# HGRN2 recurrence and SwiGLU block in fp32: the state of two heads kept as diagonal blocks over 128 rows

## The chip, the cores and the metric

The kernel runs on one core of a Trainium2 chip. The metric is the device time of one execution in microseconds (us); the figure of a kernel is the median of its runs.

## What is computed

Four sequences (batch) of 768 tokens, eight heads of 48 dimensions. Each head keeps a 48x48 state that is decayed by a gate f row by row and takes in the outer product of k and v; the output of a token is q times the state. The result, with the heads of a token side by side (384 columns, 3072 tokens), goes through a SwiGLU block with three weight matrices, which arrive in float64.

```python
q, k, v, f_logit: (4, 8, 768, 48)
f = 1.0 / (1.0 + np.exp(-f_logit))
for t in range(S):
    state = f[:, :, t, :, None] * state + np.einsum('bhd,bhe->bhde', k[:, :, t], v[:, :, t])
    y[:, :, t] = np.einsum('bhd,bhde->bhe', q[:, :, t], state)
x = y.transpose(0, 2, 1, 3).reshape(B * S, H * D)          # (3072, 384)
g = x @ w_gate                                             # (384, 1536)
out = (g * sigmoid(g) * (x @ w_val)) @ w_out               # (1536, 384)
```

## The kernel before

**Tiling.** The recurrence runs in chunks of 128 tokens, six per sequence, 24 in all (chunk u is sequence b = u // 6 and position c = u % 6). The main loop (L276 to L285) goes over the 24 chunks; `attention(u)` is a generator that yields twelve times. Three chunks make a block of 384 tokens for the SwiGLU part; `mlp(g)` returns fifteen pieces of work for block g (twelve `hidden`, three `down`), and the main loop runs one piece behind every second yield of the next block's chunks. The last chunk of a block gets only the three `down` pieces, in its first half. In chunks 0 to 2 the pieces are the eighteen conversions of float64 weights to fp32, which are work for DVE and one product on POOL. The order on each engine is set by the tile scheduler; TensorE fills what it can with the SwiGLU matmuls.

**One chunk.** Raw f, q and k stand as tokens x (8 heads x 64), the upper 16 of each 64 columns zero. Twelve transposes (L143) turn them so that two heads share the 128 partitions, rows 0 to 47 and 64 to 111, with zeros between; four such pairs (index a) lie side by side. POOL forms the products of neighbouring gates e (L193) and q times f (L168). L165 and, in seven levels, L185 form the weights A of token s in token t: 48-row matmuls, the two heads of a pair in rows 0 and 64. After a level's matmuls DVE multiplies half of qT (L188), POOL half of kT (L190) by gates, and DVE copies the level's part of the scores into A under a mask (L194). After the last level qT is q times all gates of the chunk up to the token.

**The y stage.** For each of the eight heads y is A times v (L205, a contraction over the chunk's 128 tokens) and, where c > 0, qT times the state before the chunk (L208, a contraction over the head's 48 rows). Both add up in the same PSUM columns. A head's two matmuls follow one another, so in these chunks TensorE changes between 128 rows and 48 rows at every matmul. The two heads of a pair write different PSUM banks. L210 (ACT) copies y to x.

**The state.** It is a tile of 128 x (4 pairs x 48). For chunks c < 5 kT is transposed back (L217), copied (L219) and multiplied by v into PSUM, dS (L221); DVE decays the old state (L226) and adds dS (L227), or only copies it for c = 0 (L229). Then x is transposed for the SwiGLU part (L240, L242). `hidden` is L253 to L258, `down` L263 to L268. Loads are issued by SyncE two chunks ahead.

Of the kernel before, what the change touches and what calls it, by code (L numbers as in the profile page):

```python
# [8 lines left out]
FP32 = mybir.dt.float32  # L9
# [3 lines left out]
ALU = mybir.AluOpType  # L13
# [3 lines left out]
def kernel(  # L17
# [10 lines left out]
):  # L28
    """Gated linear recurrence over chunks of 128 tokens, then a SwiGLU block, all in fp32.

    Within a chunk the weight of token s in token t is the product of the gates of s+1..t. It is
    formed level by level: at level m the chunk splits into blocks of 2m tokens, and pairs with s
    in a block's left half and t in its right half take (product from s to the middle) times
    (product from the middle to t). Both are products of gates, so nothing exceeds 1 whatever the
    gates are, and nothing is divided. From a level to the next, q's right halves and k's left
    halves take the product of the neighbour half's gates.

    Two heads share the partitions, 64 apart; the two parities of head use different PSUM banks.
    """
    nc = tc.nc  # L40
# [3 lines left out]
    HP = H // 2  # L44
# [19 lines left out]

# [1 line left out]
    ident = const.tile([128, 128], FP32, tag="ident", name="ident")  # L66
    make_identity(nc, ident)
    masks = {}
    for m in LEVELS:
        mk = const.tile([128, 64], I32, tag=f"mask{m}", name=f"mask{m}")  # L70
        # s - (first token of t's block of 2m): within [0, m) where s is in its left half
        nc.gpsimd.iota(mk, pattern=[[-2 * m, 64 // m], [0, m]], base=0, channel_multiplier=1)
        nc.vector.tensor_single_scalar(mk, mk, ~(m - 1), op=ALU.bitwise_and)
        nc.vector.tensor_single_scalar(mk, mk, 0, op=ALU.is_equal)
        masks[m] = mk
# [10 lines left out]

# [1 line left out]
    units = [(b, c) for b in range(B) for c in range(NCH)]  # L88
# [10 lines left out]
    def weight_pieces(dst, src):  # L99
        """Fills dst (fp32) from src in pieces. A float64 comes as two int32 words, low first, and  # L100
        is rounded to fp32 here: sign and exponent make a power of two (0 below fp32's normal
        range, inf above it), which takes 1 + the mantissa's two parts."""
        n0, n1 = dst.shape[1:]
# [24 lines left out]

# [1 line left out]
    state = {}  # L130
    xT = {}

    def rows_of(par):
        return slice(W * par, W * par + D)

    def attention(u):
# [21 lines left out]

        # s = t
        A = att.tile([128, H, C], FP32, tag="A", name="A")  # L160
# [11 lines left out]

        # s < t, level by level
        E = fT
# [24 lines left out]

        # y: within the chunk, and from the state before it  # L200
        y = aps.tile([128, 2, 512], FP32, tag="a", name="y")
        for a in range(HP):
            for par in range(2):
                o = y[:, par, a * D:(a + 1) * D]
                nc.tensor.matmul(o, lhsT=A[:, par * HP + a, :], rhs=vt[u][:, 2 * a + par, :], start=True, stop=(c == 0))  # L205
                if c:
                    r = rows_of(par)
                    nc.tensor.matmul(o, lhsT=qT[r, a, :], rhs=state[b, c - 1][r, a, :], start=False, stop=True)  # L208
        x = att.tile([128, HP, 2, D], FP32, tag="x", name="x")
        nc.scalar.copy(x.rearrange("t a r d -> t r a d"),  # L210
                       y[:, :, 0:HP * D].rearrange("t r (a d) -> t r a d", d=D))
        yield

        if c < NCH - 1:
            p = aps.tile([128, 2, 512], FP32, tag="a", name="dS")
            for a in range(HP):
                nc.tensor.transpose(p[:, 0, a * C:(a + 1) * C], kT[:, a, :], ident)  # L217
            kt = att.tile([128, H, W], FP32, tag="kt", name="kt")
            nc.scalar.copy(kt, p[:, 0].rearrange("t (h d) -> t h d", d=W))  # L219
            for h in range(H):  # L220
                nc.tensor.matmul(p[W * (h % 2):W * (h % 2) + W, 1, (h // 2) * D:(h // 2 + 1) * D],  # L221
                                 lhsT=kt[:, h, :], rhs=vt[u][:, h, :], start=True, stop=True)
            s = att.tile([128, HP, D], FP32, tag="state", name="state", bufs=3)
            dS = p[:, 1, 0:HP * D].rearrange("p (a d) -> p a d", d=D)
            if c:
                nc.vector.tensor_tensor(s, state[b, c - 1], E.broadcast_to((128, HP, D)), ALU.mult)  # L226
                nc.vector.tensor_tensor(s, s, dS, ALU.add)  # L227
            else:
                nc.vector.tensor_copy(s, dS)  # L229
            state[b, c] = s  # L230
        yield

        # x.T for the block of tokens
        g = u // GROUP
# [9 lines left out]

# [1 line left out]
    def mlp(g):  # L246
# [24 lines left out]

# [1 line left out]
    for u in range(AHEAD):  # L273
# [46 lines left out]
```

## Time and profile before

| | |
|---|---|
| median of 3 runs | 1224.22 us (1221.59 to 1225.0) |
| span of the profiled execution | 1223.5 us (the page gives no other time of it) |
| TensorE busy | 1104.9 us, 90% |
| VectorE (DVE), GpSimd (POOL), ScalarE (ACT) busy | 34%, 22%, 14% |

The span is from the first to the last instruction of one execution. PE is TensorE's matmuls and PEld its weight loads. An fp32 matmul stands as two records, so `x2` in the timeline is one matmul and `x16` eight; a transpose is one record. A duration in the timeline runs from the first start to the last end of a merged group; the pace is read from the starts, since the end of a matmul is modelled. PEclk is the clock that TensorE was granted, as a share of 2.4 GHz; it has two levels, 1.00 and 0.50, and a mean over a stretch can lie between.

### The profile page before, as it was taken

The page shows a single profiled execution, that of the slowest core. Times are in us where ns is not written, and L with a number is a line of the kernel's source. Part 1 is how long each engine was busy: PE and PEld are TensorE (multiplying, and loading weights), DVE is VectorE, ACT ScalarE, POOL GpSimd, SP SyncE. Part 2 cuts the span into 40 slices and gives each one's busy share as a digit, 9 for nine tenths or more (in the row PEclk, how much of TensorE's full clock was granted, in tenths as well). Part 3 has the DMA queues.
Part 4 walks back from the last instruction along what each step waited for, and adds up shares of the span by engine and source line. Part 5 has one row for each costly group of instructions (what it writes and reads, how often), then busy time and mean ns, then how long its engine had stood idle before and what let it go on. Part 6 is the DMA issues. An engine that isn't in the chain of part 4 may idle for free.

```text
span 1223.5 us, 14949 instructions
## 1 busy us (share of the span) xinstructions
PE 1104.9 (90%) x6264; PEld 761.0 (62%) x6264; DVE 421.3 (34%) x656; ACT 166.7 (14%) x288; POOL 267.4 (22%) x400
## 2 busy tenths in 40 slices
PE   3546599998999999998999989998999989998998
PEld 3545566666666576666666666665666666665654
DVE  5997952321432222421332222412232213322110
ACT  1101022010121011210121110210121110110010
POOL 3454331111221121311221221211221211211000
PEclk9955588896998978988898968989798969989799
DMA  9534211010011010110110110110110100000000
GB/s 196 130 113 113 68 26 27 1 39 19 15 27 26 20 27 7 20 33 13 27 27 7 33 33 1 27 26 20 27 27 1 40 7 1 1 1 20 1 1 19
DMA packets 106721, 38.69 MB, mean 32 GB/s; under 512 B 100512, under 2 KB 103584, under 8 KB 106656
## 3 DMA queue, kind: packets, MB, share of 16 engines
q1 hardware_dynamic: 103200, 33.04, 12.4%
q10 hardware_dynamic: 3456, 4.72, 1.1%
q8 instruction: 49, 0.80, 0.3%
q14 instruction: 16, 0.13, 0.0%
HBM read 33.03 MB, written 4.72 MB: 31 GB/s over the span
## 4 chain that ended last, share of the span: by engine, by line
PE 84%; DVE 11%; issue 3%; POOL 1%; ACT 0%; DMA 0%; SPq 0%; DVEq 0%; POOLq 0%; ACTq 0%
PE gate L253 17%; PE val L253 16%; PE o L263 15%; PE sc L185 14%; PE y L205 7%; PE y L208 7%; DVE A L194 3%; DVE qT L188 2%; PE fkT L143 2%; PE sc L165 2%; PE dS L221 1%; PE dS L217 1%; DVE p L116 1%; PE xTp L240 1%; PE qTp L143 1%
## 5 line engine op out<-in xcount | busy, mean ns | idle before, releaser
L185 PEld LDWEIGHTS sc<-qT,kT 48*128 48x128 f32 x2688 | 188.2, 211 | 156.9 <-issue 79.8
L185 PE MATMUL sc<-qT,kT 48*128 48x64 f32 x2688 | 211.6, 302 | 78.2 <-DVE A L194 56.3
L253 PE MATMUL gate<-xT,w_gate 128*128 128x384 f32 x576 | 244.2, 538 | 0.6 <-ACT xT L242 0.6
L253 PE MATMUL val<-xT,w_val 128*128 128x384 f32 x576 | 216.1, 514 | 0.0
L190 POOL TENSOR_TENSOR kT<-kT,e 128x256 f32<-128x256 f32 x144 | 118.1, 820 | 393.4 <-PE sc L185 393.4
L263 PE MATMUL o<-w_out,h 128*128 128x384 f32 x576 | 197.0, 493 | 1.1 <-ACT ob L266 1.1
L253 PEld LDWEIGHTS val<-xT,w_val 128*128 128x128 f32 x576 | 117.6, 204 | 86.1 <-issue 14.6
L258 DVE TENSOR_TENSOR h<-silu,val 128x384 f32<-128x384 f32 x96 | 53.2, 554 | 317.5 <-PE val L253 317.5
L263 PEld LDWEIGHTS o<-w_out,h 128*128 128x128 f32 x576 | 105.8, 190 | 69.8 <-ACT ob L266 2.4
L194 DVE COPY_PREDICATED A<-mask,sc 128x512 f32<-128x512 int32 x168 | 147.0, 875 | 0.0
L188 DVE TENSOR_TENSOR qT<-qT,e 128x256 f32<-128x256 f32 x144 | 63.3, 440 | 213.4 <-PE sc L185 213.1
L253 PEld LDWEIGHTS gate<-xT,w_gate 128*128 128x128 f32 x576 | 101.4, 200 | 45.2 <-issue 4.4
L205 PE MATMUL y<-v,A 128*128 128x48 f32 x384 | 99.5, 364 | 16.7 <-issue 16.7
L205 PEld LDWEIGHTS y<-v,A 128*128 128x128 f32 x384 | 77.4, 258 | 33.6 <-issue 22.9
L193 POOL TENSOR_TENSOR e<-fT 128x256 f32<-128x256 f32 x24 | 15.1, 629 | 361.2 <-ACT fT L150 361.2
L256 ACT ACTIVATE silu<-gate 128x384 f32<-128x384 f32 x96 | 47.1, 490 | 336.9 <-PE gate L253 336.9
L208 PE MATMUL y<-state,qT 48*128 48x48 f32 x320 | 92.1, 380 | 0.0
L208 PEld LDWEIGHTS y<-state,qT 48*128 48x128 f32 x320 | 68.3, 265 | 12.4
L210 ACT COPY x<-y 128x384 f32<-128x384 f32 x24 | 11.5, 478 | 367.7 <-PE y L208 322.2
L193 POOL TENSOR_TENSOR e<-e 128x128 f32<-128x128 f32 (+1 forms) x144 | 41.3, 287 | 9.5
L190 POOL TENSOR_TENSOR kT<-kT,fT 128x256 f32<-128x256 f32 x24 | 23.7, 988 | 80.8 <-PE sc L185 80.8
L266 ACT COPY ob<-o 128x384 f32<-128x384 f32 x24 | 11.5, 478 | 213.8 <-PE o L263 213.8
(50 smaller groups left out, 598.0 us busy)
## 6 DMA issues: line engine op xcount, KB each, us to landing
fraw<-in_f_logit_dram SPq DMA_DIRECT2D x24, 192.0 KB, 3.0
qraw<-in_q_dram SPq DMA_DIRECT2D x24, 192.0 KB, 3.8
kraw<-in_k_dram SPq DMA_DIRECT2D x24, 192.0 KB, 4.1
v<-in_v_dram SPq DMA_DIRECT2D x24, 192.0 KB, 2.6
w<-in_moe_w_gate_dram SPq DMA_DIRECT2D x6, 768.0 KB, 5.6
w<-in_moe_w_val_dram SPq DMA_DIRECT2D x6, 768.0 KB, 4.3
w<-in_moe_w_out_dram SPq DMA_DIRECT2D x6, 768.0 KB, 4.4
out_dram<-ob ACTq DMA_DIRECT2D x24, 192.0 KB, 1.9
```

The source lines that it names most:

```text
L143: nc.tensor.transpose(dst[:, a * C:(a + 1) * C], src[:, 2 * a:2 * a + 2, :].rearrange("t r d -> t (r d)"), ident)
L185: nc.tensor.matmul(sc[:, par, o + 64 * a:o + 64 * a + 64].rearrange("p (n r) -> p n r", r=m), lhsT=kT[r, a, :], rhs=qv[r, a, :, 1, :], sta ...
L188: nc.vector.tensor_tensor(qv[:, :, :, 1, :], qv[:, :, :, 1, :], ev[:, :, :, 0:1].broadcast_to((128, HP, n, m)), ALU.mult)
L190: nc.gpsimd.tensor_tensor(kv[:, :, :, 0, :], kv[:, :, :, 0, :], ev[:, :, :, 1:2].broadcast_to((128, HP, n, m)), ALU.mult)
L193: nc.gpsimd.tensor_tensor(E, ev[:, :, :, 0], ev[:, :, :, 1], ALU.mult)
L194: nc.vector.copy_predicated(A.rearrange("p g (n two r) -> p g n two r", two=2, r=m)[:, :, :, 1, :], masks[m].rearrange("p (n r) -> p n r", ...
L205: nc.tensor.matmul(o, lhsT=A[:, par * HP + a, :], rhs=vt[u][:, 2 * a + par, :], start=True, stop=(c == 0))
L208: nc.tensor.matmul(o, lhsT=qT[r, a, :], rhs=state[b, c - 1][r, a, :], start=False, stop=True)
L253: nc.tensor.matmul(dst, lhsT=w[:, i, j * 128:(j + 1) * 128], rhs=xT[g][:, i, :], start=(i == 0), stop=(i == KT - 1))
L256: nc.scalar.activation(sg, gp, AF.Silu)
L258: nc.vector.tensor_tensor(h[j], sg, vp, ALU.mult)
L263: nc.tensor.matmul(op, lhsT=h[j][:, s * C:(s + 1) * C], rhs=w_out[:, j, :], start=(j == 0), stop=(j == NF - 1))
```

## The change

The state of a pair is kept as a 128 x 96 block with the two heads' 48x48 states on its diagonal and zeros elsewhere. One matmul over all 128 rows then gives the state's part of y for both heads (96 columns), and A times v adds to its halves. All y matmuls contract over 128 rows and write one PSUM bank. The decay of the state, now 128x384, goes from DVE to POOL; DVE adds dS to the two diagonal halves in two operations of 64 rows. The three state tiles are fixed and set to zero once. (Comments taken out by the diff are left out here. Line numbers of the changed kernel are higher by up to 7: L205 and L208 become L212 and L209, L227 becomes L234, L226 becomes L230.)

```diff
+    states = [const.tile([128, HP, 2, D], FP32, tag=f"state{i}", name=f"state{i}") for i in range(3)]
+    for s in states:
+        nc.gpsimd.memset(s, 0.0)
     state = {}
     xT = {}
...
         y = aps.tile([128, 2, 512], FP32, tag="a", name="y")
         for a in range(HP):
+            both = y[:, 0, 2 * a * D:2 * (a + 1) * D]
+            if c:
+                nc.tensor.matmul(both, lhsT=qT[:, a, :], rhs=state[b, c - 1][:, a, :, :].rearrange("p r d -> p (r d)"),
+                                 start=True, stop=False, skip_group_check=True)
             for par in range(2):
-                o = y[:, par, a * D:(a + 1) * D]
-                nc.tensor.matmul(o, lhsT=A[:, par * HP + a, :], rhs=vt[u][:, 2 * a + par, :], start=True, stop=(c == 0))
-                if c:
-                    r = rows_of(par)
-                    nc.tensor.matmul(o, lhsT=qT[r, a, :], rhs=state[b, c - 1][r, a, :], start=False, stop=True)
+                nc.tensor.matmul(both[:, par * D:(par + 1) * D], lhsT=A[:, par * HP + a, :], rhs=vt[u][:, 2 * a + par, :],
+                                 start=(c == 0), stop=True, skip_group_check=True)
         x = att.tile([128, HP, 2, D], FP32, tag="x", name="x")
-        nc.scalar.copy(x.rearrange("t a r d -> t r a d"),
-                       y[:, :, 0:HP * D].rearrange("t r (a d) -> t r a d", d=D))
+        nc.scalar.copy(x.rearrange("t a r d -> t (a r d)"), y[:, 0, 0:DM])
         yield
 
         if c < NCH - 1:
...
             for h in range(H):
                 nc.tensor.matmul(p[W * (h % 2):W * (h % 2) + W, 1, (h // 2) * D:(h // 2 + 1) * D],
                                  lhsT=kt[:, h, :], rhs=vt[u][:, h, :], start=True, stop=True)
-            s = att.tile([128, HP, D], FP32, tag="state", name="state", bufs=3)
+            s = states[u % len(states)]
             dS = p[:, 1, 0:HP * D].rearrange("p (a d) -> p a d", d=D)
             if c:
-                nc.vector.tensor_tensor(s, state[b, c - 1], E.broadcast_to((128, HP, D)), ALU.mult)
-                nc.vector.tensor_tensor(s, s, dS, ALU.add)
-            else:
-                nc.vector.tensor_copy(s, dS)
+                nc.gpsimd.tensor_tensor(s, state[b, c - 1], E.unsqueeze(2).broadcast_to((128, HP, 2, D)), ALU.mult)
+            for par in range(2):
+                half = slice(W * par, W * par + W)
+                if c:
+                    nc.vector.tensor_tensor(s[half, :, par, :], s[half, :, par, :], dS[half], ALU.add)
+                else:
+                    nc.vector.tensor_copy(s[half, :, par, :], dS[half])
             state[b, c] = s
```

**TensorE around y, a chunk with c > 0 and SwiGLU work beside it (chunk 3).** In rows of the order, `128x48 x2` is two matmuls with 48 moving columns. Before:

```order
L253 MATMUL val<-xT,w_val 128x384 x3
L185 MATMUL sc_1059<-qT,kT 128x64 x8
L253 MATMUL gate<-xT,w_gate 128x384 x2
L205 MATMUL y<-v,A 128x48
L208 MATMUL y<-state,qT 128x48
...
L253 MATMUL gate<-xT,w_gate 128x384
L253 MATMUL val<-xT,w_val 128x384 x3
L217 MATMUL dS<-ident,kT 128x128 x4
```

Now:

```order
L260 MATMUL val<-xT,w_val 128x384 x3
L189 MATMUL sc_1057<-qT,kT 128x64 x8
L260 MATMUL gate<-xT,w_gate 128x384
L209 MATMUL y<-state_129,qT 128x96
L260 MATMUL gate<-xT,w_gate 128x384
L212 MATMUL y<-v,A 128x48 x2
...
L260 MATMUL gate<-xT,w_gate 128x384
L260 MATMUL val<-xT,w_val 128x384 x3
L221 MATMUL dS<-ident,kT 128x128 x4
```

The pair of rows L205, L208 stood eight times; now L209 and `L212 x2` stand four times. The first state matmul has moved ahead of one of the two gate matmuls that stood before y.

**POOL at the start of chunk 2**, where it forms the gate products e and q times f (`w_val`, `w_out` are weight conversions). Before:

```order
L193 TENSOR_TENSOR e_780<-e_753 128x16
L193 TENSOR_TENSOR e_793<-e_780 128x8
L193 TENSOR_TENSOR e_820<-e_793 128x4
L168 TENSOR_TENSOR qT<-q_661,fT 128x512
L125 TENSOR_TENSOR w_val<-man,p_626 128x768
L125 TENSOR_TENSOR w_out<-man,p_678 128x768
L190 TENSOR_TENSOR kT<-kT,fT 128x256
```

Now:

```order
L197 TENSOR_TENSOR e_782<-e_755 128x16
L197 TENSOR_TENSOR e_795<-e_782 128x8
L197 TENSOR_TENSOR e_822<-e_795 128x4
L230 TENSOR_TENSOR state_129<-state_128,e_822 128x384
L172 TENSOR_TENSOR qT<-q_663,fT 128x512
L125 TENSOR_TENSOR w_val<-man,p_628 128x768
L125 TENSOR_TENSOR w_out<-man,p_680 128x768
```

The decay stands behind the last e and, in chunks 1 to 3, ahead of the first product of qT; in later chunks that product stands earlier and the decay is the last before the first product of kT.

**DVE at the end of chunk 1**, between two weight pieces and the next chunk's copy of kT. Before:

```order
L119 SCALAR_TENSOR_TENSOR p_590<-w_588,p_590 128x768
L226 TENSOR_TENSOR state<-state,e_566 128x192
L116 TENSOR_SCALAR p_626<-w_624 128x768
L227 TENSOR_TENSOR state<-state,dS 128x192
L117 TENSOR_SCALAR p_626<-p_626 128x768
...
L124 SCALAR_TENSOR_TENSOR man<-w_624,man 128x768
L152 COPY kT<-fkT 128x512
```

Now:

```order
L119 SCALAR_TENSOR_TENSOR p_592<-w_590,p_592 128x768
L234 TENSOR_TENSOR state_128<-state_128,dS 64x4x48 x2
L116 TENSOR_SCALAR p_628<-w_626 128x768
L121 TENSOR_SCALAR top<-w_626 128x768
L117 TENSOR_SCALAR p_628<-p_628 128x768
...
L119 SCALAR_TENSOR_TENSOR p_628<-w_626,p_628 128x768
L156 COPY kT<-fkT 128x512
```

The decay L226 is gone, the sum is two operations, and the first operation of the next weight piece (L116) has moved from ahead of the sum to behind it. In both the sum stands ahead of the copy of kT.

## Rows read from the trace of the kernel before

**Rows 1.** The page: TensorE's line of the busy table; granted clock in forty slices of 30.6 us.
```profile
PE 1104.9 (90%) x6264; PEld 761.0 (62%) x6264; DVE 421.3 (34%) x656; ACT 166.7 (14%) x288; POOL 267.4 (22%) x400
...
PEclk9955588896998978988898968989798969989799
```

**Rows 2.** The page: the chain that ended last, by line.
```profile
PE gate L253 17%; PE val L253 16%; PE o L263 15%; PE sc L185 14%; PE y L205 7%; PE y L208 7%; DVE A L194 3%; DVE qT L188 2%; PE fkT L143 2%; PE sc L165 2%; PE dS L221 1%; PE dS L217 1%; DVE p L116 1%; PE xTp L240 1%; PE qTp L143 1%
```

**Rows 3.** Timeline, TensorE, chunk 4: start us, length us, instruction, count.
```profile
235.13 0.42 PE L208 MATMUL y<-state,qT 48*128 48x48 f32 x2
235.48 0.42 PE L205 MATMUL y<-v,A 128*128 128x48 f32 x2
...
238.29 0.66 PE L205 MATMUL y<-v,A 128*128 128x48 f32 x2
238.88 0.66 PE L208 MATMUL y<-state,qT 48*128 48x48 f32 x2
...
241.83 1.65 PE L253 MATMUL gate<-xT,w_gate 128*128 128x384 f32 x2
```

**Rows 4.** Timeline, TensorE, chunk 6 (c = 0).
```profile
333.81 1.92 PE L205 MATMUL y<-v,A 128*128 128x48 f32 x16
335.56 0.88 PE L253 MATMUL gate<-xT,w_gate 128*128 128x384 f32 x2
```

**Rows 5.** Stretches: length, busy us (records) by engine, clock, DMA share, GB/s.
```profile
234.89:238.20 3.31, 3.31 (x21) 2.82 (x20) 0.00 (x0) 0.00 (x0) 0.00 (x0) 1.00 0.00 0
238.25:241.83 3.58, 3.58 (x13) 2.99 (x13) 0.00 (x0) 0.00 (x0) 0.00 (x0) 0.50 0.00 0
...
333.80:335.60 1.80, 1.80 (x18) 1.80 (x17) 0.00 (x0) 0.00 (x0) 0.00 (x0) 1.00 0.00 0
```

**Rows 6.** Stretches from y's first matmul to the next transpose: chunks 3, 7, 22, 6.
```profile
189.64:206.43 16.79, 16.79 (x77) 11.51 (x76) 0.91 (x2) 2.43 (x5) 0.00 (x0) 0.80 0.06 12
...
372.10:390.33 18.23, 18.23 (x76) 12.57 (x76) 0.91 (x2) 2.42 (x5) 0.00 (x0) 0.72 0.06 12
...
1077.98:1094.62 16.64, 16.64 (x77) 11.68 (x77) 0.91 (x2) 2.43 (x5) 0.00 (x0) 0.79 0.00 1
333.81:343.65 9.84, 9.84 (x61) 6.76 (x61) 0.91 (x2) 2.43 (x5) 0.00 (x0) 1.00 0.11 22
```

**Rows 7.** Stretches: the y stage of chunks 1 and 23, to TensorE's next work.
```profile
95.55:104.97 9.42, 9.42 (x33) 7.96 (x33) 5.69 (x9) 0.00 (x0) 3.24 (x2) 0.50 0.25 84
...
1135.22:1145.27 10.05, 9.48 (x33) 7.96 (x33) 0.00 (x0) 0.48 (x1) 0.00 (x0) 0.50 0.00 0
```

**Rows 8.** Timeline, chunk 5's end and the next chunk's transposes, at half clock.
```profile
291.31 0.72 DVE L194 COPY_PREDICATED A<-mask,sc 128x512 f32<-128x512 int32 x1
...
292.13 0.63 PE L205 MATMUL y<-v,A 128*128 128x48 f32 x2 [1.27 <-issue]
...
302.88 1.06 PE L143 MATMUL fkT<-ident,fraw 128*128 128x128 f32 x4
...
303.73 1.06 PE L143 MATMUL fkT<-ident,kraw 128*128 128x128 f32 x4
```

**Rows 9.** Timeline, DVE and POOL, from chunk 1's end into chunk 2.
```profile
100.69 0.55 DVE L116 TENSOR_SCALAR p<-w 128x768 int32<-128x768 int32 x1
...
107.95 0.35 DVE L227 TENSOR_TENSOR state<-state,dS 128x192 f32<-128x192 f32 x1 [6.71 <-PE dS L221]
...
114.58 1.57 POOL L168 TENSOR_TENSOR qT<-q,fT 128x512 f32<-128x512 f32 x1
...
120.98 1.11 DVE L188 TENSOR_TENSOR qT<-qT,fT 128x256 f32<-128x256 f32 x1
```

**Rows 10.** Groups by line and shape, POOL: busy us, mean ns, idle before.
```profile
L190 POOL TENSOR_TENSOR kT<-kT,e 128x256 f32<-128x256 f32 x144 | 118.1, 820 | 393.4 <-PE sc L185 393.4
...
L168 POOL TENSOR_TENSOR qT<-q,fT 128x512 f32<-128x512 f32 x24 | 31.0, 1293 | 0.0
```

**Rows 11.** Timeline, POOL, the first product of kT in chunk 6.
```profile
312.41 0.84 POOL L190 TENSOR_TENSOR kT<-kT,fT 128x256 f32<-128x256 f32 x1 [3.13 <-PE sc L185]
```

## The prediction

> **What bounds the kernel now.** I read the page's table of engines and its forty slices first, then the chain of waits, then the timeline of TensorE around one stage, and last the granted clock of single stretches. TensorE is busy for 90% of the span, and its clock line falls to half (the 5s and 6s) again and again after the start [rows 1]. In the chain TensorE has most of the span, and the two lines of the y stage, L205 and L208, have 7% each [rows 2]. So what TensorE spends in y is on the path that sets the end, as long as it has other work queued or is itself waited for.
>
> A matmul is two records in the trace, a transpose one; times below are per record. In a chunk with c > 0 the sixteen y matmuls alternate: two records over 128 rows (L205), two over 48 (L208). From one matmul to the next 0.35 us pass (235.13 to 235.48), later in the same stage 0.59 us (238.29 to 238.88) [rows 3]. In a chunk with c = 0 only the 128-row ones exist: sixteen records start at 333.81 and the next work at 335.56, so 1.75 us, 0.109 us a record, against 0.175 in the alternation [rows 4]. The stage of chunk 4, which begins at 234.89, is thus 6.94 us long (to 241.83), four times the 1.75 us for twice the records. The step from 0.35 to 0.59 is the clock: it was granted in full up to 238.20 and at half behind that, with TensorE busy in all of both stretches; in chunk 6 it stayed at full [rows 5]. So the alternation costs twice: each matmul is slower, and what follows runs at 1.2 instead of 2.4 GHz for a while.
>
> **What the change does to TensorE.** Of sixteen y matmuls in each of the twenty chunks with c > 0 twelve are left, all over 128 rows: 24 records where 32 were, and the alternation is gone. The state's matmul moves 96 columns instead of 48. A 128-row record with 48 columns takes 0.109 us at full clock (above); the transposes, with 128 columns, take 0.85 / 4 = 0.2125 us at half clock (302.88 to 303.73) [rows 8], and half of that is 0.106. Both ends of the column count give the same, so 96 costs no more than 48. The new stage: 24 x 0.109 = 2.62 us at full clock, 24 x 0.2125 = 5.10 at half.
>
> Eleven chunks have SwiGLU matmuls around their y. From y's first matmul to the next chunk's first transpose they take 16.79 (first) to 16.64 us (last); two of them, at 372.10 and 470.71, take 18.2. TensorE is busy all the time, at a mean clock of 0.72 to 0.80. Chunk 6 with c = 0 does the same work, less the state's matmuls, in 9.84 at full clock [rows 6]. I take 9.84 + 8 x 0.109 = 10.7 for all eleven, which assumes that the clock stays up as it does there. Before: 9 x 16.7 + 2 x 18.2 = 186.7. After: 11 x 10.7 = 117.7. **Gain 69.0 us**; about two thirds of it are y itself and one third the half clock behind it.
>
> Nine chunks (1, 2 and the last of each block) have y wholly at half clock, since the levels before it have gaps: first matmul to next work 9.42 us at 95.55, and 10.05 at 1135.22, of which TensorE is busy for 9.48; the rest, a wait for the copy of x, stays [rows 7]. With 5.10 instead of 9.42, 4.3 x 9 = **38.9 us**. The half clock behind these stages I leave as it is. Here TensorE also waits 1.27 us for A's last update (DVE, to 292.03) before y begins [rows 8]; the first state matmul now stands ahead of A's and needs only qT, which DVE finishes before that update. Its two records (0.43 us) go into the wait: 0.43 x 9 = **3.8 us**.
>
> **What it does to the others.** The decay of the state goes from DVE to POOL and doubles to 128x384. No row has it; POOL's products of 128x256 take 0.82 us and of 128x512 1.29 [rows 10], and I take 1.05, midway as its size is. It is issued after the e products and before the first kT product, and there POOL waits 3.13 us for TensorE [rows 11], so I cost it at nothing from chunk 4 on. There are sixteen (c from 1 to 4); uncovered they would cost up to 16 x 1.29 = 21 us. In chunks 1 to 3 it stands ahead of qT's first product, which TensorE's first level needs; but DVE, busy with the weights, gets to its part of that level only at 120.98, and POOL's longer work may hold DVE up by its own length. I charge 1 us in chunks 1 and 2 each. Bounds: 0 and 1.57, the length of qT's product there [rows 9].
>
> On DVE the decay goes (0.35 us) and the sum over 128x192 becomes two over 64 rows. The row has 0.35 for one [rows 9]; for half the rows I take the same, since the elements per row are the same, with zero and twice that as bounds. In chunks 1 and 2 DVE now waits at the sum, 6.71 us, for TensorE's dS [rows 9], so y's gain shortens that wait and counts in full. In exchange the first operation of a weight piece moves behind the sum, ahead of the copy of kT: 0.55 + 0.35 = about 1 us in each of the two chunks. **Loss, all told: 4 us.** Three memsets of 128x384 on POOL come before its first product, which waits for the first transposes and their copy: nothing. The ACT copy of x reads the same 384 columns from one bank instead of two: nothing, TensorE has SwiGLU work beside it. No DMA moves.
>
> **Sum.** 69.0 + 38.9 + 3.8 - 4 = 107.7. The profiled span is 1223.5, and the page gives no other time of that execution; the median of the runs, 1224.22, lies 0.7 above. 1223.5 - 107.7 + 0.7 = 1116.5, so **1116 us**.
>
> **Rivals.**
> *The clock falls all the same.* In the eleven chunks y runs at half clock, 5.10, and what follows takes what it takes now (chunk 4: 16.63 - 6.94 = 9.7): 14.8 instead of 10.7, 4.1 x 11 = 45 us less gain, **1161**. Against it: chunk 6, with the same dense records, kept the full clock [rows 5], and so did its whole stretch [rows 6]. For it: the new stage is half as long again as chunk 6's. 0.08. The Trainium skill, "TensorE: Matmul & The Clock Gate", section "HAM oscillation — how this bites in real kernels", ties the clock's fall to idle gaps of the engine. By that rule the alternation, which has no gap, would not be what lowers it, and removing it would not bring the clock back. The trace disagrees: the fall is inside a stretch with TensorE busy throughout [rows 5].
>
> *The weight loads don't overlap.* If 128-row records of different matmuls cost what they cost in the alternation, 0.175 at full and 0.295 at half clock, the stage takes 4.2 or 7.1: 11 x 1.58 + 9 x 1.98 = 35 us less, **1151**. Against it stand sixteen records in 1.75 us. 0.04. The same page of the Trainium skill, section "Part 3: Packing small matmuls — row/col tiling", says that a weight load overlaps matmuls in flight only when its row group differs; by it 128-row matmuls, which all share the rows, would be the slow case and the 48-row ones the quick one, which speaks against this change. [Rows 4] do not bear it out.
>
> *POOL's decay is not covered.* 21 us less gain, **1137**. 0.04.
>
> *It gets slower.* POOL's queue is in order: the decay waits for DVE's sums of the chunk before, these for dS, and behind it stand the kT products that every level needs. If level one then waited as long as DVE waits for dS in chunk 1, 6.71 us, and for the decay itself, 1.05, the sixteen chunks would lose 124 and the time would be 1116 + 124 = **1240**; it decides from 107.7 / 16 = 6.7 us a chunk. Against it: DVE's sums stand ahead of its copy of kT, without which no level starts, so the wait ends before it is felt. 0.02.
>
> *More than forecast.* The denser stage keeps or regains the full clock in the nine chunks too: 2.62 for 5.10, 22 us more, **1094**. 0.04.
>
> That the alternation stays is no case: the order of TensorE shows four matmuls of 96 and eight of 48 columns, and the code takes all 128 rows.
>
> **Numbers.** My forecast has 0.78, its own range 1106 to 1128 (the nine stages' clock, the start and the two odd stretches). The range of 8 in 10 takes in the uncovered decay above, with some room, and most of the regained clock below: 1098 to 1142. Faster by over 0.3%, about what a measurement of this kernel can tell from no change: all cases but the slow one and a rest, 0.97; within 0.3% 0.01; slower 0.02.
>
> **What would show it.** Right: y stages of about 2.6 us in eleven chunks and 5.1 in nine; a granted clock of 1.00 from y to the next transpose in the eleven; 10.7 us for that stretch; POOL still waiting for TensorE at level one. Wrong: a clock of 0.5 inside or behind y in the eleven; records of the new lines over 0.12 us at full clock; TensorE waiting for kT or for DVE's sums; chunks 1 and 2 that are not some 2 to 5 us shorter each.

## The result, and the profile after

The changed kernel takes 1121.05 us (median of 4 runs, 1120.33 to 1121.79) beside 1222.9 for the kernel before on the same chip: a ratio of 0.9166 [0.9143, 0.9188]. The forecast was 1116, with 1098 to 1142 around it. The profiled execution took 1120.95 us, with a span of 1119.0 where before had 1223.5: 104.5 us less, against 107.7 in the forecast's sum. A run that lies over 1.5% above the fastest of its kernel is left out of the ratios; of all the runs below that is one, the longest of e5_pairs.

The page of the changed kernel, TensorE's line of the busy table, the granted clock, and the chain by line (compare [rows 1, 2]):

```profile
PE 995.0 (89%) x6104; PEld 686.2 (61%) x6104; DVE 434.0 (39%) x660; ACT 166.6 (15%) x288; POOL 281.2 (25%) x419
...
PEclk9955579997999979998899979999899979999899
...
PE gate L260 17%; PE val L260 16%; PE o L270 16%; PE sc L189 15%; PE y L212 5%; DVE A L198 4%; DVE qT L192 3%; PE y L209 3%; PE fkT L147 2%; PE sc L169 2%; PE dS L225 1%; DVE man L124 1%; DVE p L116 1%; PE dS L221 1%; PE xTp L247 1%
```

TensorE is busy for 110 us less (995.0 for 1104.9) with only 160 records fewer. The clock line has no 5 or 6 behind the start, where before it fell again and again. In the chain, y has gone from 14% (L205, L208) to 8% (L212, L209). Of DVE's entries two have grown: its copy into A (3% to 4%) and its products of qT (2% to 3%). They turn out to be the part that the prediction missed.

The y stage of chunk 4 (compare [rows 3]), timeline of TensorE, to the first transpose of chunk 5:

```profile
221.63 0.37 PE L209 MATMUL y<-state,qT 128*128 128x96 f32 x2
221.84 0.84 PE L260 MATMUL gate<-xT,w_gate 128*128 128x384 f32 x2
222.51 0.54 PE L212 MATMUL y<-v,A 128*128 128x48 f32 x4
222.89 0.43 PE L209 MATMUL y<-state,qT 128*128 128x96 f32 x2
223.15 0.57 PE L212 MATMUL y<-v,A 128*128 128x48 f32 x4
...
224.90 0.88 PE L260 MATMUL gate<-xT,w_gate 128*128 128x384 f32 x2
...
232.98 0.38 PE L147 MATMUL fkT<-ident,fraw 128*128 128x128 f32 x2
```

The stage lasts 3.27 us (221.63 to 224.90). One gate matmul lies inside it, as the order showed; it takes 0.67 of that (221.84 to 222.51), so y's 24 records take 2.60. The state's matmul with 96 columns goes at the pace of those with 48: six records from 222.51 to 223.15 (0.64 us).

Stretches of chunk 4 behind y's first matmul, and the last part of chunk 5 with its half-clock stage (compare [rows 5 to 7]); columns as in [rows 5]:

```profile
222.51:224.90 2.39, 2.39 (x24) 2.39 (x22) 0.00 (x0) 0.00 (x0) 0.00 (x0) 1.00 0.00 0
224.90:232.98 8.08, 8.08 (x45) 5.00 (x45) 1.26 (x3) 2.42 (x5) 0.00 (x0) 1.00 0.12 24
...
271.93:278.64 6.71, 5.58 (x26) 5.27 (x24) 1.06 (x2) 0.48 (x1) 0.85 (x1) 0.50 0.01 2
```

In chunk 4 the clock stays at 1.00 from y to the next transposes, and that stretch, less the gate matmul, takes 10.7 us (11.35 - 0.67). All eleven chunks show 11.34 or 11.35. In chunk 5 the stage is still at half clock.

### The profile page after: what moved, and what is told of

Same layout as the page of the kernel before. It is cut to its first block, busy times and chain, and to the rows that moved or that the text cites. A ratio compares the mean times of both kernels' runs of the same rounds, so it can differ in the third digit from the quotient of the medians.

```text
span 1119.0 us, 14668 instructions
## 1 busy us (share of the span) xinstructions
PE 995.0 (89%) x6104; PEld 686.2 (61%) x6104; DVE 434.0 (39%) x660; ACT 166.6 (15%) x288; POOL 281.2 (25%) x419
## 4 chain that ended last, share of the span: by engine, by line
PE 82%; DVE 14%; issue 2%; POOL 1%; ACT 0%; DMA 0%; SPq 0%; DVEq 0%; POOLq 0%; ACTq 0%
PE gate L260 17%; PE val L260 16%; PE o L270 16%; PE sc L189 15%; PE y L212 5%; DVE A L198 4%; DVE qT L192 3%; PE y L209 3%; PE fkT L147 2%; PE sc L169 2%; PE dS L225 1%; DVE man L124 1%; DVE p L116 1%; PE dS L221 1%; PE xTp L247 1%
## 5 line engine op out<-in xcount | busy, mean ns | idle before, releaser
L189 PE MATMUL sc<-qT,kT 48*128 48x64 f32 x2688 | 210.2, 301 | 89.0 <-DVE A L198 65.5
L260 PE MATMUL gate<-xT,w_gate 128*128 128x384 f32 x576 | 234.9, 518 | 0.6 <-ACT xT L249 0.6
L194 POOL TENSOR_TENSOR kT<-kT,e 128x256 f32<-128x256 f32 x144 | 121.2, 842 | 400.6 <-PE sc L189 400.6
L260 PE MATMUL val<-xT,w_val 128*128 128x384 f32 x576 | 201.9, 486 | 0.0
L260 PEld LDWEIGHTS val<-xT,w_val 128*128 128x128 f32 x576 | 109.6, 190 | 76.5 <-issue 0.6
L260 PEld LDWEIGHTS gate<-xT,w_gate 128*128 128x128 f32 x576 | 96.9, 193 | 40.0 <-issue 2.3
L212 PE MATMUL y<-v,A 128*128 128x48 f32 x384 | 70.4, 323 | 2.7 <-issue 2.7
L212 PEld LDWEIGHTS y<-v,A 128*128 128x128 f32 x384 | 67.7, 249 | 8.1 <-issue 4.0
L209 PE MATMUL y<-state,qT 128*128 128x96 f32 x160 | 43.9, 366 | 8.0 <-DVE qT L192 8.0
L192 DVE TENSOR_TENSOR qT<-qT,fT 128x256 f32<-128x256 f32 x24 | 26.0, 1084 | 53.5 <-PE sc L189 53.5
L173 DVE TENSOR_TENSOR A<-sc,ident 128x1024 f32<-128x1024 f32 x24 | 29.4, 1223 | 35.7 <-PE sc L169 35.7
```

The source lines that it names most:

```text
L173: nc.vector.tensor_tensor(A, sc.rearrange("p r (a t) -> p (r a) t", t=C), ident.unsqueeze(1).broadcast_to((128, H, C)), ALU.mult)
L189: nc.tensor.matmul(sc[:, par, o + 64 * a:o + 64 * a + 64].rearrange("p (n r) -> p n r", r=m), lhsT=kT[r, a, :], rhs=qv[r, a, :, 1, :], sta ...
L192: nc.vector.tensor_tensor(qv[:, :, :, 1, :], qv[:, :, :, 1, :], ev[:, :, :, 0:1].broadcast_to((128, HP, n, m)), ALU.mult)
L194: nc.gpsimd.tensor_tensor(kv[:, :, :, 0, :], kv[:, :, :, 0, :], ev[:, :, :, 1:2].broadcast_to((128, HP, n, m)), ALU.mult)
L209: nc.tensor.matmul(both, lhsT=qT[:, a, :], rhs=state[b, c - 1][:, a, :, :].rearrange("p r d -> p (r d)"), start=True, stop=False, skip_gro ...
L212: nc.tensor.matmul(both[:, par * D:(par + 1) * D], lhsT=A[:, par * HP + a, :], rhs=vt[u][:, 2 * a + par, :], start=(c == 0), stop=True, sk ...
```

## Level one of the weights: what the prediction had not looked at

Both traces at level one in chunk 4. Before:

```profile
211.99 0.36 DVE L226 TENSOR_TENSOR state<-state,e 128x192 f32<-128x192 f32 x1 [3.12 <-POOL e L193]
212.26 1.22 DVE L169 TENSOR_TENSOR A<-sc,ident 128x1024 f32<-128x1024 f32 x1
213.40 0.55 DVE L258 TENSOR_TENSOR h<-silu,val 128x384 f32<-128x384 f32 x1
214.15 0.43 DVE L188 TENSOR_TENSOR qT<-qT,fT 128x256 f32<-128x256 f32 x1 [0.21 <-PE sc L185]
214.19 1.09 POOL L190 TENSOR_TENSOR kT<-kT,fT 128x256 f32<-128x256 f32 x1 [2.24 <-PE sc L185]
214.49 1.31 DVE L194 COPY_PREDICATED A<-mask,sc 128x512 f32<-128x512 int32 x1
215.95 1.11 PE L185 MATMUL sc<-qT,kT 48*128 48x64 f32 x16 [0.36 <-DVE A L194]
```

After:

```profile
198.72 0.83 POOL L230 TENSOR_TENSOR state<-state,e 128x384 f32<-128x384 f32 x1
200.88 0.84 POOL L194 TENSOR_TENSOR kT<-kT,fT 128x256 f32<-128x256 f32 x1 [1.34 <-PE sc L189]
200.90 1.10 DVE L192 TENSOR_TENSOR qT<-qT,fT 128x256 f32<-128x256 f32 x1 [0.49 <-PE sc L189]
201.92 1.28 DVE L198 COPY_PREDICATED A<-mask,sc 128x512 f32<-128x512 int32 x1
203.34 1.11 PE L189 MATMUL sc<-qT,kT 48*128 48x64 f32 x16 [1.07 <-DVE A L198]
```

Both products wait for the same matmuls and start 0.02 to 0.04 us apart. Whichever starts first runs quickly, and the other pays: DVE 0.43 and POOL 1.09 in before's chunk 4, POOL 0.84 and DVE 1.10 in after's. DVE's copy into A stands behind its product, and TensorE's next level waits for that copy, 0.36 us before and 1.07 now. In before, DVE's product came 0.04 us ahead and took 0.43 us in 13 of the 24 chunks, the same 13 in which its decay had waited for POOL's last e. In after it takes 0.43 us in none. In chunks 1 to 3 of after DVE does start ahead of POOL's kT product, but POOL is then still at a weight product, and DVE's is slow all the same (chunk 2):

```profile
118.01 1.80 POOL L125 TENSOR_TENSOR w_out<-man,p 128x768 f32<-128x768 f32 x1 [1.76 <-DVE p L119]
118.99 1.11 DVE L192 TENSOR_TENSOR qT<-qT,fT 128x256 f32<-128x256 f32 x1
119.78 1.02 POOL L194 TENSOR_TENSOR kT<-kT,fT 128x256 f32<-128x256 f32 x1
```

A semaphore is how one engine tells another that its work is done; the waits for semaphores that the trace keeps for each instruction show where the lead comes from. POOL's product starts 0.068 us behind the signal of the last matmul. DVE's starts 0.023 us behind it in the 13 chunks, where the product waits for TensorE alone, since the decay ahead of it has already waited for POOL. Without that decay the product waits for POOL too, by a second instruction, though POOL's part has been done for over 1 us in chunk 4, and it starts 0.09 us behind the signal. So one wait more, 0.07 us, decides which engine is first; from chunk 4 on it is so in every trace here in which the edit does not hold POOL back.

The groups by line and shape show the slower product and the longer wait for the whole kernel; before, then after:

```profile
L188 DVE TENSOR_TENSOR qT<-qT,fT 128x256 f32<-128x256 f32 x24 | 17.4, 725 | 45.1 <-PE sc L185 45.1
L185 PE MATMUL sc<-qT,kT 48*128 48x64 f32 x2688 | 211.6, 302 | 78.2 <-DVE A L194 56.3 <-POOL kT L190 11.0 <-DVE qT L188 8.8
```

```profile
L192 DVE TENSOR_TENSOR qT<-qT,fT 128x256 f32<-128x256 f32 x24 | 26.0, 1084 | 53.5 <-PE sc L189 53.5
L189 PE MATMUL sc<-qT,kT 48*128 48x64 f32 x2688 | 210.2, 301 | 89.0 <-DVE A L198 65.5 <-POOL kT L194 11.0 <-DVE qT L192 8.8
```

The mean of the 24 products went from 725 to 1084 ns, and TensorE's wait for A from 56.3 to 65.5 us. That is 13 x 0.7 = 9 us, which the prediction did not charge.

## Experiments

**Theory:** the gain comes from the alternation of row counts in y, through the pace of the records and through the clock. **Rivals:** it comes from fewer matmuls, or from the state's form and its handling on POOL and DVE. A second question is whether the 9 us at level one come from the decay's move.

**e1_grouped.** The kernel before, with only the order of its sixteen y matmuls changed: the eight of A first, then the eight of the state over 48 rows. In this kernel the state's part takes the place of A's part in some columns of y, since every A matmul sets the start flag of its bank.

```diff
         for a in range(HP):
             for par in range(2):
                 o = y[:, par, a * D:(a + 1) * D]
-                nc.tensor.matmul(o, lhsT=A[:, par * HP + a, :], rhs=vt[u][:, 2 * a + par, :], start=True, stop=(c == 0))
-                if c:
+                nc.tensor.matmul(o, lhsT=A[:, par * HP + a, :], rhs=vt[u][:, 2 * a + par, :], start=True, stop=(c == 0),
+                                 skip_group_check=True)
+        if c:
+            for a in range(HP):
+                for par in range(2):
+                    o = y[:, par, a * D:(a + 1) * D]
                     r = rows_of(par)
-                    nc.tensor.matmul(o, lhsT=qT[r, a, :], rhs=state[b, c - 1][r, a, :], start=False, stop=True)
+                    nc.tensor.matmul(o, lhsT=qT[r, a, :], rhs=state[b, c - 1][r, a, :], start=False, stop=True,
+                                     skip_group_check=True)
```

> The kernel before with one edit: in y all eight A matmuls stand first, then all eight 48-row state matmuls; same sixteen matmuls, same state handling, two PSUM banks. Theory 'alternation': the cost lies in changing between 128 and 48 rows at every matmul. Then a stage is 16 x 0.109 + 16 x 0.065 (the pace of the 48-row records of the levels) and one change, 2.8 to 3.0 us at full clock and about 5.6 at half, the clock stays up behind y in the eleven chunks, and the time is 1110 to 1122, at or a little under the changed kernel. Rival 'the 48-row matmuls are what is slow, and the change gains by having fewer of them': all of the excess stays with them, the stage stays near 6 us, the clock falls, about 1215 to 1225. Rival 'half the excess goes': 1165 to 1180.

Measured: 1118.39 us (1117.48 to 1121.07), ratio 0.9141 [0.9127, 0.9156]. Timeline of TensorE in chunk 4:

```profile
219.68 1.88 PE L205 MATMUL y<-v,A 128*128 128x48 f32 x16
221.49 1.09 PE L212 MATMUL y<-state,qT 48*128 48x48 f32 x16
222.51 0.91 PE L258 MATMUL gate<-xT,w_gate 128*128 128x384 f32 x2
```

Stretches of the same kernel, chunk 4's y, what follows it, and chunk 5's y:

```profile
219.67:222.51 2.84, 2.84 (x33) 2.73 (x32) 0.00 (x0) 0.00 (x0) 0.00 (x0) 1.00 0.00 0
222.51:230.63 8.12, 8.12 (x45) 5.04 (x44) 0.91 (x2) 2.42 (x5) 0.00 (x0) 1.00 0.13 26
271.08:277.16 6.08, 5.50 (x33) 5.25 (x33) 0.00 (x0) 0.48 (x1) 0.00 (x0) 0.50 0.17 35
```

The same 32 records as before, in another order, take 2.84 us instead of 6.94, at full clock. So fewer matmuls and another form of the state are not needed for the gain: the order alone brings as much as the whole change. What they add is taken up at the end of the next section. The sixteen 48-row records together take 1.02 us (221.49 to 222.51), less than sixteen 128-row ones (1.81).

**e7_grouped_flag.** The same order, with the start flag on the first matmul of each bank alone, so that A's part stays (the lines are set against e1_grouped).

```diff
-                nc.tensor.matmul(o, lhsT=A[:, par * HP + a, :], rhs=vt[u][:, 2 * a + par, :], start=True, stop=(c == 0),
+                nc.tensor.matmul(o, lhsT=A[:, par * HP + a, :], rhs=vt[u][:, 2 * a + par, :], start=(a == 0), stop=(c == 0),
                                  skip_group_check=True)
```

> The kernel before with the grouped order (eight A matmuls, then eight state matmuls), and the accumulation's start flag set only on the first matmul of each PSUM bank, so that the state's part adds to A's part in all columns (with a start flag on every A matmul, as in the first grouped kernel, the later ones of a bank undo the accumulation of the earlier columns, so there the state's part replaces A's part in some columns). The flag is no instruction: same time as that kernel, 1115 to 1121. Rival 'the first kernel was quick because something was left out': nearer to 1223.

Measured: 1119.64 us (1117.44 to 1120.65), ratio 0.9156 [0.914, 0.9172]. The flag costs nothing that can be told, and an order and a flag alone reach the time of the whole change (0.9166 [0.9143, 0.9188]).

**e2_state_only.** The other half: the changed kernel, its 128x96 state, POOL's decay and all, with before's alternating y stage put back.

```diff
-            if c:
-                nc.tensor.matmul(both, lhsT=qT[:, a, :], rhs=state[b, c - 1][:, a, :, :].rearrange("p r d -> p (r d)"),
-                                 start=True, stop=False, skip_group_check=True)
             for par in range(2):
...
+                o = y[:, par, a * D:(a + 1) * D]
+                nc.tensor.matmul(o, lhsT=A[:, par * HP + a, :], rhs=vt[u][:, 2 * a + par, :], start=True, stop=(c == 0))
+                if c:
+                    r = rows_of(par)
+                    nc.tensor.matmul(o, lhsT=qT[r, a, :], rhs=state[b, c - 1][r, a, par, :], start=False, stop=True)
...
```

> The changed kernel with the y stage of before: sixteen matmuls in alternation, the 48-row ones reading the diagonal blocks; the state stays a block of 128x96, its decay on POOL, the sum in two halves on DVE. Theory: TensorE's gain goes entirely (stages of 6.4 to 7.4 us, clock falling in y), and what the state's handling costs by itself shows: the first qT product of twelve chunks comes behind POOL's kT product, 12 x 0.7 us, so 1228 to 1236. Rival 'the state's handling costs nothing': 1219 to 1226. Rival 'it is part of the gain': below 1215.

Measured: 1224.67 us (1222.62 to 1226.67, 10 runs), ratio 1.0013 [1.0001, 1.0025]. That is not the 1228 to 1236 expected; by the time alone it is the rival's 1219 to 1226, the state's handling costing nothing. But level one lost what was expected:

```profile
L189 PE MATMUL sc<-qT,kT 48*128 48x64 f32 x2688 | 209.0, 300 | 88.8 <-DVE A L198 67.0 <-POOL kT L194 11.0 <-DVE qT L192 8.8
...
L192 DVE TENSOR_TENSOR qT<-qT,fT 128x256 f32<-128x256 f32 x24 | 26.0, 1083 | 53.5 <-PE sc L189 53.5
```

From its transposes to its y, chunk 4 takes 29.16 us where before took 28.46, and chunks 1 and 2 became 1.4 and 1.8 us longer. Over all chunks the stretches up to y lose 7.6 us. What makes up for it lies behind y's first matmul, 6.4 us in all: in six of the eleven stages the clock fell later than in before, in two it fell earlier (13 and 19, 1.6 us longer each). Chunk 4's y and what follows it:

```profile
238.12:243.63 5.51, 5.51 (x33) 4.64 (x32) 0.00 (x0) 0.00 (x0) 0.00 (x0) 1.00 0.00 0
243.63:253.45 9.82, 9.82 (x45) 5.78 (x45) 1.26 (x3) 2.42 (x5) 0.00 (x0) 0.83 0.11 22
```

Here the alternation runs its whole 5.51 us at full clock and the clock falls only behind it. This splits the two costs: at full clock the alternating records take 5.51 us where the grouped ones take 2.84, and the fall adds to that. Why it falls later here than in before is not shown. The state's handling is no part of the gain; by itself it costs time, in the 7.6 us ahead of y: 0.7 us at level one in each of 13 chunks, and the longer chunks 1 and 2.

**e5_pairs.** The kernel before with its y matmuls in the order A, A, state, state for each pair: seven changes of the row count in a stage instead of fifteen.

```diff
-        for a in range(HP):
-            for par in range(2):
-                o = y[:, par, a * D:(a + 1) * D]
...
+        for a0 in range(HP):
+            for a in range(a0, a0 + 1):
+                for par in range(2):
+                    o = y[:, par, a * D:(a + 1) * D]
+                    nc.tensor.matmul(o, lhsT=A[:, par * HP + a, :], rhs=vt[u][:, 2 * a + par, :], start=True, stop=(c == 0),
+                                     skip_group_check=True)
+            if c:
+                for a in range(a0, a0 + 1):
+                    for par in range(2):
+                        o = y[:, par, a * D:(a + 1) * D]
+                        r = rows_of(par)
+                        nc.tensor.matmul(o, lhsT=qT[r, a, :], rhs=state[b, c - 1][r, a, :], start=False, stop=True,
+                                         skip_group_check=True)
```

> The kernel before with y in the order A, A, state, state for each pair of heads: half as many changes between 128 and 48 rows, all matmuls as before. Theory 'alternation', each change costing the same (about 0.18 us at full clock, 0.25 at half): stages of about 4.2 us at full and 7.4 at half clock; 47 us less if the clock falls as before, up to 70 if it stays: 1153 to 1176. Rival 'only a change at every single matmul hurts': near the grouped order, 1110 to 1130. Rival 'number and kind of the matmuls': 1215 to 1225.

Measured: 1155.76 us (1148.64 to 1166.31), ratio 0.9424 [0.939, 0.9457]; its runs spread more than those of the others, and the profile is of the longest. Stretches, the y stages of chunks 3 and 4 and what follows each:

```profile
183.04:186.66 3.62, 3.62 (x34) 3.19 (x33) 0.00 (x0) 0.00 (x0) 0.00 (x0) 1.00 0.00 0
186.66:196.47 9.81, 9.81 (x46) 5.79 (x44) 0.91 (x2) 2.42 (x5) 0.00 (x0) 0.83 0.11 22
224.92:229.03 4.11, 4.11 (x33) 3.61 (x32) 0.00 (x0) 0.00 (x0) 0.00 (x0) 0.86 0.00 0
229.03:239.93 10.90, 10.90 (x46) 6.39 (x44) 0.91 (x2) 2.42 (x5) 0.00 (x0) 0.74 0.10 20
```

In between, as the theory wants it. In this run the clock falls in all eleven chunks, at the end of y or just behind it; the other three runs have a higher mean clock (0.894 to 0.916 beside 0.885), so there it may fall less often. With one, seven and fifteen changes the stage takes 2.84, 3.62 and 5.51 us at full clock: 0.13 us for each of the first six changes and 0.24 for each of the next eight. At half clock it takes 5.43, 6.42 and 9.42. Why the last changes cost more isn't settled; in the full alternation two 48-row matmuls no longer stand side by side, and those are quick (e1_grouped), but that was not tried by itself.

**e3_decay_dve.** The changed kernel with the decay back on DVE, now over 128x384.

```diff
-                nc.gpsimd.tensor_tensor(s, state[b, c - 1], E.unsqueeze(2).broadcast_to((128, HP, 2, D)), ALU.mult)
+                nc.vector.tensor_tensor(s, state[b, c - 1], E.unsqueeze(2).broadcast_to((128, HP, 2, D)), ALU.mult)
```

> The changed kernel with the decay of the state (128x384) on DVE instead of POOL. Theory 'order at level one': in the kernel before DVE was still busy when level one's scores ended, in twelve chunks with a decay, and its qT product then came ahead of POOL's kT product (0.43 us instead of 1.10); in the changed kernel it comes behind in nearly all. With the decay back on DVE it comes first again, TensorE's wait at level one falls from about 1.07 to 0.36 us in twelve chunks: 8 us less, 1111 to 1116. Rival 'the decay on POOL is hidden and so is that wait': 1119 to 1123. Rival 'DVE's longer decay is on the path': 16 x 0.55 more, 1127 to 1131.

Measured: 1111.71 us (1110.04 to 1113.5), ratio 0.9083 [0.9068, 0.9099]. Level one of chunk 4, DVE, POOL and TensorE:

```profile
197.07 0.56 DVE L230 TENSOR_TENSOR state<-state,e 128x384 f32<-128x384 f32 x1 [3.13 <-POOL e L197]
...
199.23 0.43 DVE L192 TENSOR_TENSOR qT<-qT,fT 128x256 f32<-128x256 f32 x1
199.27 1.08 POOL L194 TENSOR_TENSOR kT<-kT,fT 128x256 f32<-128x256 f32 x1 [2.24 <-PE sc L189]
...
201.02 1.11 PE L189 MATMUL sc<-qT,kT 48*128 48x64 f32 x16 [0.36 <-DVE A L198]
```

DVE comes first again, in the same 13 chunks as in before, and TensorE's wait for A is 57.0 us instead of 65.5. The kernel is 9.3 us faster than the changed one (1121.05 - 1111.71), which is the 13 x 0.7. So the decay's move to POOL, which the prediction costed at nothing, cost 9 us, and through DVE's place in the order rather than through POOL's queue. That DVE was still busy when the scores ended, as expected here, is not how it comes first: in before's chunk 4 it stood idle for 0.21 us ahead of the product. In this run too its product waits for TensorE alone in the 13 chunks and starts 0.023 us behind the signal.

**e4_dve_first.** The changed kernel with POOL held behind DVE at level one by two small operations, the first of which reads qT.

```diff
             if m == 1:
+                turn = att.tile([128, 1], FP32, tag="turn", name="turn")
+                nc.gpsimd.tensor_single_scalar(turn, qT[:, 0, 1:2], 0.0, op=ALU.mult)
+                nc.gpsimd.tensor_tensor(kT[:, 0, 0:1], kT[:, 0, 0:1], turn, ALU.add)
```

> The changed kernel, decay on POOL as it is; at level one POOL gets two tiny operations of one column ahead of its kT product, the first of which reads qT, so that the kT product can only start behind DVE's qT product. Theory 'order at level one': DVE's product takes 0.43 instead of 1.10 us in chunks 3 to 23, TensorE's wait before level two falls by about 0.7 us in each, 21 x 0.7 = 15 us less, of which the two small operations may take back some: 1105 to 1112. Rival 'the wait only moves to POOL's kT product, which now ends later': 1117 to 1123. Rival 'the gain of the decay on DVE came from POOL's shorter queue, not from the order': 1119 to 1123.

Measured: 1113.99 us (1112.49 to 1114.22), ratio 0.9109 [0.9092, 0.9126]. Chunk 4:

```profile
201.44 0.43 DVE L192 TENSOR_TENSOR qT<-qT,fT 128x256 f32<-128x256 f32 x1 [0.49 <-PE sc L189]
...
201.96 0.21 POOL L196 TENSOR_SCALAR turn<-qT 128x1 f32<-128x1 f32 x1 [1.85 <-DVE qT L192]
202.25 0.19 POOL L197 TENSOR_TENSOR kT<-kT,turn 128x1 f32<-128x1 f32 x1
202.52 0.84 POOL L198 TENSOR_TENSOR kT<-kT,fT 128x256 f32<-128x256 f32 x1
203.41 1.11 PE L189 MATMUL sc<-qT,kT 48*128 48x64 f32 x16 [0.60 <-POOL kT L198]
```

DVE's product is at 0.43 and the wait down from 1.07 to 0.60, but it is now a wait for POOL, whose product starts 0.65 us behind the end of DVE's (201.87 to 202.52). So 7 us are gained, less than expected (the range ended at 1112). Together with e3_decay_dve it shows that the order of the two products at level one is the cause: set by another work on DVE or by a wait, DVE first is the faster.

**e6_decay_dve_first** (e3_decay_dve with the same three lines) and **e8_grouped_dve_first** (e7_grouped_flag with them):

> Both: the decay on DVE and POOL's kT product of level one behind DVE's qT product. Thirteen chunks have DVE first already by the decay; the order alone adds the other eight behind the start: 8 x 0.7 = 5.6 us under the kernel with the decay on DVE, 1104 to 1108. Rival 'two ways to one gain, and the small operations cost': 1111 to 1116.

> The grouped order with the flag on each bank's first matmul, and POOL's kT product of level one behind DVE's qT product. Thirteen chunks have DVE first by the old decay; the other eight gain 0.7 each: 5.6 us under the grouped kernel, 1110 to 1115. Rival as for the kernel with the decay on DVE: no gain, 1117 to 1122.

Measured: 1108.8 us (1107.14 to 1111.5), ratio 0.9072 [0.9053, 0.909], and 1115.91 us (1114.82 to 1118.82), ratio 0.9132 [0.9113, 0.915]. Both lie just outside the range expected, on its slow side. e6_decay_dve_first cannot be told from e3_decay_dve, whose interval overlaps its own; both are faster than the changed kernel and the one before. For e8_grouped_dve_first the step over e7_grouped_flag is 3.7 us, with intervals that touch: where DVE was first in 13 chunks already, there is little left.

## Why the prediction was right, and the term it lacked

**The eleven stretches** (forecast 186.7 to 117.7, gain 69.0). Measured 186.9 to 117.5 without the gate matmul that moved inside (11 x 10.68): 69.4. The clock stays at 1.00 [rows 5, 6], as in chunk 6. The cause holds up: e1_grouped and e7_grouped_flag get it with an order alone, and e2_state_only loses it when the alternation comes back. Nor is it that a matmul adds to PSUM columns written just ahead of it, as the state's did in before: in the changed kernel L212 does the same behind L209, at 0.109 us a record. The Trainium skill, "TensorEngine Tiling (Array Packing)", section "Key Properties", says that changing the tiling mode drains the engine; the trace agrees that changes cost, 0.13 to 0.24 us each here at full clock, though no run shows a drain as such, nor that 48 rows count as another mode.

**The nine stages and the first state matmul** (38.9 + 3.8 = 42.7). From the end of the level before to the work behind y, before took 1.27 + 10.05 in chunk 5; now it takes 6.71. Over the nine the sum falls from 101.3 to 59.4 us: 41.9. All nine stay at half clock, so the case "more than forecast" did not come.

**The start** (loss 4). Chunks 1 and 2 are 3.4 and 3.0 us shorter. Their y gained 4.7 each (12.08 to 7.35 us with the wait ahead), so the loss is 1.3 + 1.7 = 3.0.

**POOL's decay, costed at nothing.** This is the step that failed. What I had named as its cover held: the decay takes 0.83 us, less than the 1.05 assumed, and POOL still waits 1.34 us for TensorE behind it (compare [rows 10, 11]), so the rival of an uncovered decay (1137) and the slower one (1240) fell for the reasons given. But I looked only at the engine that took the work on. "On DVE the decay goes (0.35 us)" left out what its wait had been doing: with it DVE was first at level one in 13 chunks, and without it TensorE waits 0.7 us longer in each: 9 us not in the sum, shown by e3_decay_dve and e4_dve_first. One of the rows that I quoted already had DVE's product at 1.11 us [rows 9], and I did not ask why.

**The balance.** The measured terms give 69.4 + 41.9 - 3.0 - 9.1 = 99.2 where the spans differ by 104.5. The other 5 us lie in stretches between transposes and y that got shorter without an edit in them. Chunks 6 and 18, which have no state to decay or multiply, show it plainest: 30.93 to 30.22 us and 31.72 to 30.50, at a mean clock of 0.94 and 0.92 before and 0.96 in both now. That less of these stretches runs at half clock would account for it, but I have no run that isolates it. They hid over half of the missing term, and it is by this luck that 1116 came as near to 1121 as it did.

**The other rivals.** The clock did not fall all the same (1161). The rule of the Trainium skill cited with that rival, that the clock falls through idle gaps, does not account for the eleven stages: in e1_grouped and in the alternation TensorE is busy throughout by the profile, and only the alternation loses the clock. It goes with the nine others, which have a gap ahead of y (1.27 us in chunk 5) and run at half clock both before and now. That weight loads of 128-row matmuls don't overlap (1151) fell with 24 records in 2.60 us.

**What the restructured state is worth.** e3_decay_dve against e7_grouped_flag, which have the same order at level one: 1119.64 - 1111.71 = 7.9 us, or 8.9 by the ratios. The stages say the same: 10.96 against 10.68 us in each of eleven, and some 0.7 in each of nine, about 9 together. As the change was made, the decay's move gave this back, so the changed kernel stands where the order alone would have put it.

## What to carry to other kernels

Before data is laid out anew so that matmuls share a row count, try to group them by it: here the order alone gave all of the 8% that the change gave, and the new layout under 1% more once the decay stayed on DVE. When an operation is moved off an engine, ask also what its wait was holding back or letting ahead on the engine it leaves; here the price was paid several instructions further down. Where the granted clock falls with TensorE busy, look at what sort of records stand in that stretch before looking for gaps.

## What was not expected of the hardware

A strided fp32 product over 128x256 on DVE took 0.43 or 1.10 us, and POOL's beside it 1.09 or 0.84, by which of the two started 0.02 to 0.04 us earlier; and whether DVE had one semaphore wait ahead of it or two decided that. The Trainium skill, "SBUF — State Buffer", section "SBUF: two separate sides", describes a pair of ports that VectorE and GpSimd share as an exclusive lock: whoever starts first has it for the whole instruction. The traces agree that the second pays. Both lengths of DVE's product stand in the trace of before already.

The changes of the row count do not cost the same each (0.13, then 0.24 us), and sixteen 48-row records in a row, of two heads in different rows, ran at 0.064 us a record against 0.113 for the 128-row ones beside them (1.02 and 1.81 us for sixteen).
